# Planning the stores of gates and gated operands two microseconds behind VectorE's last step

## The chip, the cores and the metric

The kernel runs on one core of one Trainium2 chip. The metric is the device time of one execution in microseconds. A core has TensorE (PE: matmuls, PEld: its weight loads), VectorE (DVE), ScalarE (ACT), GpSimd (POOL) and SyncE (SP). In this kernel SP issues all transfers, one after the other, in the order in which they were written; each of the other engines also works through its instructions in one order. An instruction that waits for a semaphore holds up what stands behind it on its engine.

## The reference

```python
attn = softmax(q_c @ k_c.T / 8) @ v_c      # chunks of 64 tokens, 8 heads of 64
x  = attn as (8, 576, 512)
xn = (x - mean) / sqrt(var + 1e-6) * g_ln
x  = x + relu(xn @ w_ch1) @ w_ch2          # 512 -> 2048 -> 512
gate = sigmoid(sum_k conv_w[k] * x shifted by 4 - k tokens)   # k = 0..4, zeros ahead of each sequence
out  = (gate * (x @ w_val)) @ w_out
```

All is fp32. The kernel splits an operand into a high and a low part (`ACTIVATE` Copy, then a subtraction) and adds up three products of them.

## The kernel before, in words

The 4608 tokens are worked through in nine blocks of 512 (b = 0 to 8). For every block there is attention (units of 128 tokens, `unit`), the feed-forward part, and the convolution that makes the gate. Blocks 0 and 1 go through `ffn`. From block 2 on, the first product of the feed-forward is done by `hidden` as seven products of quadrants ("2", "1", "6", "5", "3", "7", "4") for each of four groups g, 12 matmuls of 256 columns a product (L1255). Their weights were put into DRAM (`a_dram[g, m]`) and are loaded again for each product (L1327, in the trace `late_a<-a`, in the order `late_a...<-a3_1` for group 3, part 1) into a ring of six rooms. ScalarE copies a product's sum out (`c_hh`, `c_hl`, L1347), VectorE adds another to it (L1354), and later products wait for that.

`conv(b)` runs for block b while the next block is in `hidden`. For each of four column groups f it makes the gate's sum in u_room, in one of two halves, u0 and u1, in turn: a first step on ScalarE (L1638), four on VectorE (L1645), and a store to `gate_dram` (L1658, `gd`; two transfers where the block holds the start of a sequence). The half is given to the next column group but one when the store has landed. Then `seven` makes the seven operands of the gated part's first product: high on ScalarE (L1472), low on VectorE (L1477), and a store (L1482, `x7d`), from three rooms in turn. For block 0 the same is done later, out of a copy of x in DRAM (`x2d`): `seven_again` loads quadrants into u0 and u1 (L1525) as soon as the stores of the gates there have landed, and `conv_again` makes its gates in the halves too (L1600 is its store). After block 8, `val` and `proj` do the gated part; they load the operands (L1872) and the gates (L1849).

What sets the order: nearly everything is an `Op` of a `Plan`, with engine, an estimated duration, dependences and a priority. `Plan.run` plays them through in time. An engine that is free takes the ready op of the lowest priority number, and the instructions are written in that order, so the plan's times decide the order on each engine and nothing else. An op becomes ready at the end of the last op that it depends on, plus a hop (`HOP`, 80 ns behind VectorE, 3500 behind a store or load on SP), plus that op's `more`, plus its own `slack` behind SP. `HOP` is all that a store got behind VectorE.

Of the kernel before, what the change touches and what calls it, by code (L numbers as in the profile page):

```python
# [20 lines left out]


class Op:
    __slots__ = ("eng", "dur", "fn", "deps", "pri", "left", "after", "ready", "seq", "xfer", "more", "slack")

    def __init__(self, eng, dur, fn, deps, pri, seq):
        self.eng, self.dur, self.fn, self.pri, self.seq = eng, dur, fn, pri, seq
        self.deps = [d for d in dict.fromkeys(deps) if d is not None]
        self.after, self.ready, self.xfer, self.more, self.slack = [], 0.0, None, 0.0, 0.0


class Plan:
# [23 lines left out]
    def run(self):  # L56
        for op in self.ops:
            op.left = len(op.deps)
            for d in op.deps:
                d.after.append(op)  # L60
        free = {e: 740.0 if e == "SP" else 0.0 for op in self.ops for e in op.eng}
        ready = {e: [] for e in free}
        events = []
        done = set()

        def offer(op):
            for e in op.eng:
                heapq.heappush(ready[e], (op.pri, op.seq, op))

        for op in self.ops:  # L70
            if not op.left:
                offer(op)
        t, n, moved, landed = 0.0, 0, 0.0, []
        while n < len(self.ops):
            for e in free:
                if free[e] > t:
                    continue
                q = ready[e]
                while q and q[0][2].seq in done:
                    heapq.heappop(q)  # L80
                if not q:
                    spent = self.idle(t) if self.idle and e == "PE" else None
                    if spent:
                        free[e] = t + spent
                        heapq.heappush(events, (free[e], -1, None))
                    continue
                op = heapq.heappop(q)[2]
                done.add(op.seq)
                dur = op.dur[op.eng.index(e)] if isinstance(op.dur, tuple) else op.dur
                end = t  # L90
                for x, parts in op.xfer or ():
                    flying = landed[-self.LANES :]
                    if len(flying) == self.LANES:
                        end = max(end, flying[0][0])
                    for l, _ in flying:
                        if sum(m for z, m in flying if z > end) + parts > self.RING:
                            end = max(end, l)
                    turn = self.TURN if parts == P and landed and landed[-1][1] != P else 0.0
                    end += dur
                    moved = max(end + self.LAG, moved + turn) + x  # L100
                    landed.append((moved, parts))
                if not op.xfer:
                    end = t + dur
                free[e] = end
                if len(op.eng) > 1:
                    op.fn(e)
                else:
                    op.fn()
                n += 1
                for a in op.after:  # L110
                    if op.xfer:
                        wait = moved - end
                    else:
                        wait = 0.0 if a.eng == (e,) else max(self.HOP[e], self.HOP["PE"] if "PE" in a.eng else 0.0) + op.more
                        if e == "SP":
                            wait += a.slack
                    a.ready = max(a.ready, end + wait)
                    a.left -= 1
                    if not a.left:
                        heapq.heappush(events, (a.ready, a.seq, a))  # L120
                heapq.heappush(events, (free[e], -1, None))
            if n == len(self.ops):
                break
            t = max(t, events[0][0])
            while events and events[0][0] <= t:
                op = heapq.heappop(events)[2]
                if op is not None:
                    offer(op)
# [3 lines left out]
def chunk_attention_ffn_gated_conv(  # L132
# [1299 lines left out]
    def seven(b, quad, reads, pri):  # L1432

        st, last = {}, {}
        HB = NB // 2

        def mix(to, x, y, *deps):


            def side(q):
                return [(0, HB, st["t"][:, :, :HB])] if q is None else list(quad(*q))

            def go():
                if "t" not in st:
                    st["t"] = slot("hl1", [P, 2, HB], F32, f"t{b}")
                many = side(x) if x else side(y)
                for lo, hi, _ in many:
                    o, p, r = (  # L1450
                        [a for l, h, a in side(q) if (l, h) == (lo, hi)] or [st["t"][:, :, lo:hi]]
                        for q in (to, x, y)
                    )
                    nc.vector.tensor_tensor(out=o[0], in0=p[0], in1=r[0], op=ALU.subtract)

            o = add("DVE", 760, go, list(deps), pri)
            for q in (x, y):
                if q:
                    last.setdefault(q, []).append(o)
            return o  # L1460

        def split(i, m, src, *deps):
            rt, sp = SPLITS[n_split[0] % 3], {}
            n_split[0] += 1

            def sources():
                return quad(*src) if src else [(0, HB, st["t"])]

            def high():
                sp["t"] = slot(rt, [P, 2, 2, HB], F32R, f"x7_{b}_{m}")  # L1470
                for lo, hi, a in sources():
                    nc.scalar.activation(out=sp["t"][:, 0, :, lo:hi], in_=a, func=AF.Copy)  # L1472

            def low():
                t = sp["t"]
                for lo, hi, a in sources():
                    nc.vector.tensor_tensor(  # L1477
                        out=t[:, 1, :, lo:hi], in0=a, in1=t[:, 0, :, lo:hi].bitcast(F32), op=ALU.subtract
                    )

            def store():
                nc.sync.dma_start(out=x7_dram[b, m].bitcast(F32), in_=sp["t"].bitcast(F32))  # L1482

            oh = add("ACT", 680, high, list(deps) + take(rt), pri)
            ol = add("DVE", 690, low, [oh], pri)
            x7_store[b, m] = add("SP", 1300, store, [ol], pri)
            x7_store[b, m].more = 2000.0
            hold(rt, x7_store[b, m])
            if src:
                last.setdefault(src, []).append(ol)  # L1490
            return ol

        return mix, split, last
# [77 lines left out]
    def conv_again(f):  # L1571
# [30 lines left out]
        pri = when[4 + f, KF // 2]  # L1602
# [4 lines left out]
            oa = add("DVE", 760, more(i), [oa], pri)  # L1607
        hold(rt, oa)
        conv_store[0, f] = add("SP", 728, keep, [oa], pri)
        hold(at, conv_store[0, f])  # L1610

    def conv(b):
# [19 lines left out]
        for f in range(KD if b else 0):  # L1632
            st = {}
            at = f"u{f % 2}"

            def first(f=f, st=st, at=at):
                st["acc"] = slot(at, [P, XW], F32, f"acc{b}_{f}")
                nc.scalar.activation(  # L1638
                    out=st["acc"][:, :L], in_=X[b][:, f, :L], func=AF.Copy, scale=cw_sb[:, 0, f : f + 1]
                )  # L1640

            def more(i, f=f, st=st):
                def go():
                    a = st["acc"][:, :L]
                    nc.vector.scalar_tensor_tensor(  # L1645
                        out=a,
                        in0=X[b][:, f, i : i + L],
                        scalar=cw_sb[:, i, f : f + 1],
                        in1=a,
                        op0=ALU.mult,  # L1650
                        op1=ALU.add,
                    )

                return go

            def keep(f=f, st=st):
                for lo, hi, c in segs:
                    nc.sync.dma_start(  # L1658
                        out=gate_dram[b][:, f, lo:hi], in_=st["acc"][:, c - P0 : c - P0 + hi - lo]
                    )  # L1660

            oa = add("ACT", 740, first, [oz, cw_op] + done + take(at), pri)
            for i in range(1, KT):
                oa = add("DVE", 760, more(i), [oa], pri)
            last.append(oa)
            conv_store[b, f] = add("SP", 728, keep, [oa], pri)
            hold(at, conv_store[b, f])
        if b == 0:
            x2_store[b] = add("SP", 2900, store, done, pri)
# [441 lines left out]
```

## Time and profile before

| | |
|---|---|
| median of three runs | 1070.41 us (1068.2 to 1075.63) |
| the profiled execution's own time | 1070.03 us |
| its span, from first to last instruction | 1068.2 us |
| TensorE busy | 1053.9 us, 99% |
| VectorE busy | 856.4 us, 80% |
| ScalarE busy | 540.3 us, 51% |
| DMA, mean of the 16 engines | 266 GB/s |

TensorE's granted clock is at full speed in all 40 slices of the page. The waits view says who waited for whom; the timeline lists instructions in order of time with the idle time ahead of them in brackets. For SP a row is the issue of a transfer, not the transfer.

### The profile page before, as it was taken

How to read it: one execution, taken by the hardware profiler on the slowest of the kernel's cores; microseconds unless marked ns; L12 is line 12 of the kernel's file. 1: busy time of each engine (PE TensorE's matmuls, PEld its weight loads, DVE VectorE, ACT ScalarE, POOL GpSimd, SP SyncE). 2: the span in 40 equal slices, each digit the busy share in tenths (PEclk: the TensorE clock that was granted, in tenths of full speed). 3: DMA queues.
4: the chain of work that ended last, by engine and by line, in shares of the span. 5: the costliest groups of instructions: out<-in, count | busy, mean ns of one | idle time of the engine just before them, and what ended most of it. 6: DMA issues, size and time to landing. Idle time of an engine off the chain costs nothing.

```text
span 1068.2 us, 22725 instructions
## 1 busy us (share of the span) xinstructions
PE 1053.9 (99%) x8950; PEld 951.4 (89%) x8950; DVE 856.4 (80%) x1464; ACT 540.3 (51%) x871; POOL 40.4 (4%) x77
## 2 busy tenths in 40 slices
PE   9999999999999999999999999999999999999998
PEld 8988888888899988889888898899898989999998
DVE  5888978888885888767878877878756889998785
ACT  5796634435354445445445543544443555655553
POOL 1011000000000000000000000000000000000000
PEclk9999999999999999999999999999999999999999
DMA  8995358667999899989989989998976988999852
GB/s 193 289 368 175 108 159 252 220 179 207 246 329 270 233 297 337 282 242 344 278 260 329 299 233 233 352 282 250 319 234 203 381 330 305 309 334 377 316 206 80
DMA packets 205905, 284.14 MB, mean 266 GB/s; under 512 B 99278, under 2 KB 151014, under 8 KB 205798
## 3 DMA queue, kind: packets, MB, share of 16 engines
q1 hardware_dynamic: 205798, 282.68, 84.6%
q8 instruction: 71, 1.16, 0.5%
q14 instruction: 36, 0.29, 0.1%
HBM read 207.64 MB, written 67.63 MB: 258 GB/s over the span
## 4 chain that ended last, share of the span: by engine, by line
PE 88%; DMA 4%; issue 2%; DVE 2%; ACT 2%; SPq 1%; POOL 0%; DVEq 0%; ACTq 0%; POOLq 0%
PE m L1255 24%; PE o L1255 8%; PE v L1255 8%; PE y L1034 7%; PE yA L1412 5%; PE yA L1414 5%; PE yB L1412 5%; PE yB L1414 4%; PE yA L1413 4%; PE yB L1413 4%; PE att L631 3%; PE att L604 3%; PE h L1010 3%; PE h L1012 2%; PE h L1011 2%
## 5 line engine op out<-in xcount | busy, mean ns | idle before, releaser
L1255 PEld LDWEIGHTS m<-late,late_a 128*128 128x128 f32 x2352 | 296.3, 188 | 22.5 <-DVE c_hl L1354 6.1
L1255 PE MATMUL m<-late,late_a 128*128 128x256 f32 x2352 | 303.3, 280 | 7.1 <-DMA late_a<-a 3.1
L1645 DVE SCALAR_TENSOR_TENSOR u_room<-X,cw_sb,u_room 128x516 f32<-128x516 f32 (+1 forms) x128 | 95.1, 747 | 10.4 <-ACT u_room L1638 7.9
L1034 PE MATMUL y<-hh,w 128*128 128x512 f32 x224 | 70.9, 398 | 0.0
L1354 DVE TENSOR_TENSOR c_hh<-c_hh,m 128x512 f32<-128x512 f32 x56 | 38.4, 685 | 36.6 <-PE m L1255 22.9
L1347 ACT ACTIVATE c_hh<-m 128x512 f32<-128x512 f32 x56 | 33.4, 596 | 54.9 <-PE m L1255 54.7
L1412 PE MATMUL yA<-late_h,w 128*128 128x512 f32 x148 | 59.4, 401 | 0.0
L1412 PE MATMUL yB<-late_h,w 128*128 128x512 f32 x148 | 59.0, 399 | 0.0
L1414 PE MATMUL yB<-late_h,w 128*128 128x512 f32 x148 | 58.1, 393 | 0.0
L1414 PE MATMUL yA<-late_h,w 128*128 128x512 f32 x148 | 58.0, 392 | 0.0
L1413 PE MATMUL yA<-late_h,w 128*128 128x512 f32 x148 | 58.0, 392 | 0.0
L1413 PE MATMUL yB<-late_h,w 128*128 128x512 f32 x148 | 57.8, 390 | 0.0
L1034 PEld LDWEIGHTS y<-hh,w 128*128 128x128 f32 x224 | 40.8, 188 | 8.4
L1287 ACT ACTIVATE late<-xs 128x512 fp32r<-128x512 f32 x49 | 30.4, 628 | 35.1 <-PE m L1255 20.6
L1010 PE MATMUL h<-xnt,w 128*128 128x512 f32 x112 | 45.4, 405 | 0.0
L770 POOL TENSOR_TENSOR rstd<-ve,neg_half 128x1 f32<-128x1 f32 x36 | 24.7, 687 | 541.8 <-DVE ve L750 541.4
L1012 PE MATMUL h<-xnt,w 128*128 128x512 f32 x112 | 44.2, 395 | 0.0
L1011 PE MATMUL h<-xnt,w 128*128 128x512 f32 x112 | 44.2, 394 | 0.0
L1034 PE MATMUL y<-hl,w 128*128 128x512 f32 x112 | 44.0, 393 | 0.0
L1382 ACT ACTIVATE late_h<-c_hh 128x512 fp32r<-128x512 f32 x38 | 23.9, 630 | 38.9 <-DVE c_hh L1354 38.2
L678 ACT ACTIVATE p<-p 128x512 f32<-128x512 f32 x33 | 20.8, 630 | 41.6 <-DVE p L670 23.6
L699 ACT ACTIVATE pT<-px 128x1024 uint16<-128x1024 uint16 x28 | 38.5, 1374 | 6.3 <-DMA px<-ps 6.1
(272 smaller groups left out, 2440.0 us busy)
## 6 DMA issues: line engine op xcount, KB each, us to landing
late_a<-a SPq DMA_DIRECT2D x196, 512.0 KB, 5.6
x7d<-late_x SPq DMA_DIRECT2D x42, 512.0 KB, 5.9
late_a<-x7d SPq DMA_DIRECT2D x39, 512.0 KB, 5.4
raw<-in_moe_w_ch_dram SPq DMA_DIRECT2D x32, 512.0 KB, 7.6
late<-x7d SPq DMA_DIRECT2D x24, 512.0 KB, 5.5
qk_room<-in_q_dram SPq DMA_DIRECT2D x100, 112.0 KB, 5.2
qk_room<-in_k_dram SPq DMA_DIRECT2D x100, 112.0 KB, 4.1
x7d<-x SPq DMA_DIRECT2D x21, 512.0 KB, 5.6
```

The costliest lines, as they stand in the source:

```text
L699: nc.scalar.activation(out=t.bitcast(U16).rearrange("p (x s) -> p s x", s=2), in_=st["turned"], func=AF.Copy)
L1010: nc.tensor.matmul(ps, wh, xh, start=(kk == 0), stop=False)
L1011: nc.tensor.matmul(ps, wh, xl, start=False, stop=False)
L1012: nc.tensor.matmul(ps, wl, xh, start=False, stop=(kk == KD - 1))
L1034: nc.tensor.matmul(ps, w[:, s], x, start=opens and n == 0, stop=closes and n == 2, skip_group_check=not b)
L1255: nc.tensor.matmul(ps[:, f], l, right(r, k), start=new and f == k == i == 0, stop=k == 1 and i == 2, skip_group_check=True,)
L1347: nc.scalar.activation(out=st[tag], in_=st[into], func=AF.Copy)
L1354: nc.vector.tensor_tensor(out=st[tag], in0=st[tag], in1=y, op=op)
L1412: nc.tensor.matmul(ps, wh, hh, start=opens and f == 0, stop=False)
L1413: nc.tensor.matmul(ps, wl, hh, start=False, stop=False)
L1414: nc.tensor.matmul(ps, wh, hl, start=False, stop=closes and f == 3)
L1645: nc.vector.scalar_tensor_tensor(out=a, in0=X[b][:, f, i : i + L], scalar=cw_sb[:, i, f : f + 1], in1=a, op0=ALU.mult, op1=ALU.add,)
```

## The change

An op gets a number `behind`, 0 where none is set. The plan adds it where the op waits for one of an engine other than SP. It is set to 2000 ns for three kinds of stores: the operands of the gated part (`x7_store`, in `seven`), block 0's gates (`conv_again`) and the other blocks' gates (`conv`). What the kernel computes and how many instructions it has stay the same; only the plan's times change, and with them the order.

```diff
@@ class Op
-        self.after, self.ready, self.xfer, self.more, self.slack = [], 0.0, None, 0.0, 0.0
+        self.after, self.ready, self.xfer, self.more, self.slack, self.behind = [], 0.0, None, 0.0, 0.0, 0.0
@@ Plan.run
                         if e == "SP":
                             wait += a.slack
+                        else:
+                            wait += a.behind
@@ seven
             x7_store[b, m] = add("SP", 1300, store, [ol], pri)
+            x7_store[b, m].behind = 2000.0
             x7_store[b, m].more = 2000.0
@@ conv_again
         conv_store[0, f] = add("SP", 728, keep, [oa], pri)
+        conv_store[0, f].behind = 2000.0
@@ conv
             conv_store[b, f] = add("SP", 728, keep, [oa], pri)
+            conv_store[b, f].behind = 2000.0
```

What it moves, at three places. The first is SP in the convolution of block 5, while block 6 is in group 2. Before:

```order
L1482 DMA x7d5_2_120<-late_x7_1_1_3132 128x1024
L1327 DMA late_a2_0_2_2135<-a3_2_207 128x1024
L1658 DMA gd5_80<-u_room_185 128x320
L1658 DMA gd5_80<-u_room_185 128x192
L1327 DMA late_a2_0_6_2162<-a3_1_208 128x1024
L1482 DMA x7d5_6_122<-x7_5_6_7962 128x1024
L1327 DMA late_a2_0_6_2162<-a3_6_209 128x1024
```

and of the change (line numbers are two to four higher):

```order
L1484 DMA x7d5_2_120<-late_x7_1_1_3132 128x1024
L1329 DMA late_a2_0_2_2135<-a3_2_207 128x1024
L1329 DMA late_a2_0_6_2162<-a3_1_208 128x1024
L1329 DMA late_a2_0_6_2162<-a3_6_209 128x1024
L565 DMA qk_room_148<-in_q_dram 32x4x224 x4
L1662 DMA gd5_80<-u_room_185 128x320
L1662 DMA gd5_80<-u_room_185 128x192
L1484 DMA x7d5_6_122<-x7_5_6_7976 128x1024
```

The last gate store of block 5 has moved behind two weight loads and the loads of q. The second place is VectorE, ahead of the step that closes `c6_1_hl0` (block 6, group 1; the rows with X5 are gate steps of block 5). Before:

```order
L1354 TENSOR_TENSOR c6_1_hh1_7679<-c6_1_hh1_7679,m5_6_1_7686 128x512
L1645 SCALAR_TENSOR_TENSOR u_room_185<-X5_5931,cw_sb_74,u_room_185 128x516 x2
L1354 TENSOR_TENSOR c6_1_hl0_7719<-c6_1_hl0_7719,m1_6_1_7628 128x512
L1385 SCALAR_TENSOR_TENSOR h6_1_0_7673<-c6_1_hh1_7679,h6_1_0_7672 128x2x256
L669 TENSOR_REDUCE mx31_7821<-att31_7769 128x8
```

and of the change:

```order
L1356 TENSOR_TENSOR c6_1_hh1_7679<-c6_1_hh1_7679,m5_6_1_7686 128x512
L1649 SCALAR_TENSOR_TENSOR u_room_185<-X5_5934,cw_sb_74,u_room_185 128x516
L1356 TENSOR_TENSOR c6_1_hl0_7721<-c6_1_hl0_7721,m1_6_1_7628 128x512
L1387 SCALAR_TENSOR_TENSOR h6_1_0_7672<-c6_1_hh1_7679,h6_1_0_7671 128x2x256
L671 TENSOR_REDUCE mx31_7819<-att31_7768 128x8
```

One of the two gate steps has moved further down. The third place is the convolution of block 2, where `seven_again` begins (block 3, groups 2 and 3). On SP, before:

```order
L1658 DMA gd2_77<-u_room_185 128x128
L1658 DMA gd2_77<-u_room_185 128x384
L1327 DMA late_a2_0_2_2135<-a3_2_207 128x1024
L1525 DMA u_room_185<-x2d_84 128x2x256
L1658 DMA gd2_77<-u_room_185 128x128
L1658 DMA gd2_77<-u_room_185 128x384
L1327 DMA late_a2_0_6_2162<-a3_1_208 128x1024
L1482 DMA x7d2_6_101<-late_x7_1_1_3132 128x1024
L1482 DMA x7d2_3_103<-x7_2_3_4672 128x1024
L1327 DMA late_a2_0_6_2162<-a3_6_209 128x1024
L1482 DMA x7d2_4_105<-late_x7_1_1_3132 128x1024
L1327 DMA late_a2_0_3_2489<-a3_5_210 128x1024
```

and of the change:

```order
L1329 DMA late_a2_0_2_2135<-a3_2_207 128x1024
L1662 DMA gd2_77<-u_room_185 128x128
L1662 DMA gd2_77<-u_room_185 128x384
L1528 DMA u_room_185<-x2d_84 128x2x256
L1329 DMA late_a2_0_6_2162<-a3_1_208 128x1024
L1662 DMA gd2_77<-u_room_185 128x128
L1662 DMA gd2_77<-u_room_185 128x384
L1528 DMA u_room_185<-x2d_84 128x2x256
L1329 DMA late_a2_0_6_2162<-a3_6_209 128x1024
L1484 DMA x7d2_6_101<-late_x7_1_1_3132 128x1024
```

Both loads of x2d now follow the gate stores of the same rooms at once; before, the second one came six transfers after its store (it is the row behind the last that is shown). On VectorE at the same place, before (t0 and x7_0_1 read what the two loads bring; mx20 to ve19 are attention):

```order
L1385 SCALAR_TENSOR_TENSOR h3_2_1_4766<-m1_3_2_4599,h3_2_1_4765 128x2x256
L669 TENSOR_REDUCE mx20_4818<-att20_4773 128x8
L670 TENSOR_TENSOR p20_4817<-att20_4773,mx20_4818 128x2x4x64
L722 TENSOR_SCALAR rs19_4559<-rs19_4559 128x8
L723 RECIPROCAL rs19_4559<-rs19_4559 128x8
L740 TENSOR_TENSOR x19_4834<-att20_4773,rs19_4559 128x2x4x64
L747 BN_STATS stat19_4837<-x19_4834 128x6
L749 BN_AGGR mv19_4835<-stat19_4837 128x2
L750 TENSOR_SCALAR ve19_4839<-mv19_4835 128x1
L1454 TENSOR_TENSOR t0_4866<-u_room_185 128x512
L1477 TENSOR_TENSOR x7_0_1_4864<-u_room_185,x7_0_1_4864 128x512
L1354 TENSOR_TENSOR c3_3_hh0_4768<-c3_3_hh0_4768,m2_3_3_4851 128x512
```

and of the change:

```order
L1387 SCALAR_TENSOR_TENSOR h3_2_1_4766<-m1_3_2_4599,h3_2_1_4765 128x2x256
L1479 TENSOR_TENSOR late_x7_1_1_3132<-t2_4409,late_x7_1_1_3132 128x512
L1456 TENSOR_TENSOR t0_4827<-u_room_185 128x512
L1479 TENSOR_TENSOR x7_0_1_4822<-u_room_185,x7_0_1_4822 128x512
L671 TENSOR_REDUCE mx20_4838<-att20_4773 128x8
L672 TENSOR_TENSOR p20_4837<-att20_4773,mx20_4838 128x2x4x64
L1479 TENSOR_TENSOR late_x7_1_1_3132<-t0_4827,late_x7_1_1_3132 128x512
```

t0 and x7_0_1 have moved from behind the attention steps to ahead of them.

## Rows read from the trace of the kernel before

**Rows 1.** The page: span, and busy time of each engine.

```profile
span 1068.2 us, 22725 instructions
PE 1053.9 (99%) x8950; PEld 951.4 (89%) x8950; DVE 856.4 (80%) x1464; ACT 540.3 (51%) x871; POOL 40.4 (4%) x77
```

**Rows 2.** Waits of TensorE, 235 to 870 us: total us, times, longest us.

```profile
PE m L1255 <- DMA late_a<-a: 3.1, 2, 1.6
PE m L1255 <- DVE c_hl L1354: 2.1, 3, 1.0
PE m L1255 <- DVE hl L1022: 1.4, 1, 1.4
PE m L1255 <- DVE c_hh L1354: 0.5, 1, 0.5
```

**Rows 3.** Waits of SP's queue, 235 to 870 us.

```profile
SPq L1327 <- PE m L1255: 139.0, 92, 4.1
...
SPq L1482 <- DVE late_x L1477: 9.8, 12, 1.8
SPq L1658 <- DVE u_room L1645: 9.7, 7, 2.4
...
SPq L1525 <- DMA gd<-u_room: 3.3, 1, 3.3
```

**Rows 4.** Timeline of SP, 645 to 680 us: start us, us, what.

```profile
667.95 0.59 SPq L1327 DMA_DIRECT2D late_a<-a  x1
670.99 0.86 SPq L1658 DMA_DIRECT2D gd<-u_room  x2
671.95 0.44 SPq L1327 DMA_DIRECT2D late_a<-a  x1
```

**Rows 5.** Timeline of all engines, 650 to 657 us; idle time in brackets.

```profile
654.07 1.55 DVE L1645 SCALAR_TENSOR_TENSOR u_room<-X,cw_sb,u_room 128x516 f32<-128x516 f32 x2 [2.58 <-ACT u_room L1638]
...
656.27 0.97 PE L1255 MATMUL m<-late,late_a 128*128 128x256 f32 x6 [0.78 <-DVE c_hl L1354]
```

**Rows 6.** Timeline of TensorE, 555 to 566 us.

```profile
563.51 1.68 PE L1255 MATMUL m<-late,late_a 128*128 128x256 f32 x12 [0.38 <-DVE c_hl L1354]
```

**Rows 7.** Timeline of SP, 380 to 402 us.

```profile
383.28 1.10 SPq L1658 DMA_DIRECT2D gd<-u_room  x2
384.47 1.48 SPq L1327 DMA_DIRECT2D late_a<-a  x1
389.31 0.38 SPq L1525 DMA_DIRECT2D u_room<-x2d  x1
389.78 0.89 SPq L1658 DMA_DIRECT2D gd<-u_room  x2
390.77 0.42 SPq L1327 DMA_DIRECT2D late_a<-a  x1
...
395.96 0.45 SPq L1525 DMA_DIRECT2D u_room<-x2d  x1
```

**Rows 8.** Line 1525, the loads of x2d: first and last start, landing.

```profile
L1525 SPq DMA_DIRECT2D u_room<-x2d x4: 376/442/997, 389.3 to 425.1; - x4
...
DMA to landing us min/median/max: 6.9/7.3/7.7
```

**Rows 9.** Line 1658, the gate stores: landing.

```profile
DMA to landing us min/median/max: 2.5/4.7/7.6
```

**Rows 10.** Timeline of TensorE, 390 to 425 us.

```profile
396.87 2.98 PE L1255 MATMUL m<-late,late_a 128*128 128x256 f32 x24 [1.61 <-DMA late_a<-a]
...
412.88 1.54 PE L1255 MATMUL m<-late,late_a 128*128 128x256 f32 x12
...
421.06 1.68 PE L1255 MATMUL m<-late,late_a 128*128 128x256 f32 x12
```

**Rows 11.** Timeline of VectorE, 399 to 424 us.

```profile
401.12 0.68 DVE L669 TENSOR_REDUCE mx<-att 128x8 f32<-128x512 f32 x1
...
404.63 0.69 DVE L1454 TENSOR_TENSOR t<-u_room 128x512 f32<-128x512 f32 x1
```

More of the change, by code (lines that the diff above doesn't have):

```diff
@@ L23 @@
 class Op:
-    __slots__ = ("eng", "dur", "fn", "deps", "pri", "left", "after", "ready", "seq", "xfer", "more", "slack")
+    __slots__ = ("eng", "dur", "fn", "deps", "pri", "left", "after", "ready", "seq", "xfer", "more", "slack", "behind")
     def __init__(self, eng, dur, fn, deps, pri, seq):
```

## The prediction

> **What bounds the kernel now.** I read the page first: the profiled execution spans 1068.2 us and TensorE is busy for 1053.9 of it [rows 1]. So 14.3 us are without a matmul. A change that only moves instructions can't shorten the 1053.9: the matmuls are the same in number and shape. It can only take away, or add, time in which TensorE waits.
>
> Second, the waits of TensorE between 235 and 870 us, the stretch of the blocks 2 to 8, in which the gates and the operands of the gated part are made [rows 2]. There are four rows, 3.1 + 2.1 + 1.4 + 0.5 = 7.1 us. The 1.4 us, for hl of L1022, belong to block 1's plain feed-forward; the new order leaves every row up to there as it was. That leaves 5.7 us that the change could remove at best: 1070.03 - 5.7 = 1064.3.
>
> Third, the waits of the transfer queue in the same stretch [rows 3]. SP issues everything in one order. Most of its waiting is for rooms that TensorE has to free (L1327, 139.0 us), which is wanted. The rest is what the change is about: stores of gates stand waiting for VectorE's last step (L1658, 9.7 us in 7 times, 2.4 at most), and so do stores of operands (L1482, 9.8 us in 12 times). While SP stands at such a store, the weight loads (late_a) behind it are not issued.
>
> **What the change does to the plan.** No work is added or removed. In the planner's reckoning each of these stores becomes ready 2000 ns later behind VectorE. Whatever else is ready by then is put ahead of it, on SP and, because u0 and u1 come free later, on VectorE and ScalarE too. I went through the places where TensorE waits now and looked in the new order for what stands there.
>
> *Place one, 668 to 678 us (the first pieces of the order shown above).* The load of a3_1 is issued at 671.95, behind a gate store that SP holds from 668.5 (667.95 plus 0.59) to 670.99 [rows 4]. TensorE waits for it: the two waits for late_a are 3.1 us, the longest 1.6 [rows 2], and this is the other one, 1.5. In the new order the loads of a3_2, a3_1 and a3_6 follow each other and the gate store comes behind them. SP then issues a3_1 at about 668.6 (667.95 plus 0.6), some 3.3 us earlier. That covers 1.5 twice. **Gain 1.5.**
>
> *Place two, 654 to 656 us.* ScalarE's first step of a gate waits for the landing of the gate store before, VectorE's next two steps of that gate start at 654.07 and take 1.55, and only then comes c_hl, for which TensorE waits 0.78 [rows 5]. In the new order one of the two steps stands ahead of c_hl, not two. c_hl comes 1.55 / 2 = 0.78 earlier. **Gain 0.7.** The same happens a block earlier: of four gate steps ahead of c_hl two are left, and two operand steps take VectorE's idle time before them. TensorE waits there for c_hh, 0.5 [rows 2], and for c_hl, 0.38 [rows 6]. c_hh still has to come behind a gate step whose store is now issued one load later, so I keep its wait; the 0.38 goes. **Gain 0.4** (bounds: nothing and 0.9).
>
> *Place three, 383 to 422 us: the cost.* Here two loads of x2d into u_room (L1525) have to wait until the gate stores that read u_room have landed. Before: gate pair issued at 383.28 to 384.38, load of a3_2 to 385.95, then SP stands 3.3 us until 389.31 [rows 3, 7], so this store took 4.9 us to land. The median of all gate stores is 4.7 (2.5 to 7.6) [rows 9]. Then a gate pair, then the load of a3_1 at 390.77. TensorE waits 1.61 us for it [rows 10]. The second load of x2d goes out at 395.96 with six transfers between it and its store: it hardly waits.
>
> In the new order the load of a3_2 is ahead of the gate pair, and each x2d load is directly or one load behind its store. Step by step: a3_2 is issued between 383.2 (SP is free then) and 384.47 (as before) and takes 1.48, the pair 1.10, landing 4.9, so the first x2d load goes out at 390.7 to 392.0 instead of 389.31. With 0.4 for it, the load of a3_1 ends its issue at 391.6 to 392.9 against 391.19. TensorE's wait of 1.61 grows by 0.4 to 1.7; I take **1.0 lost**. Then the second pair (0.89), landing 4.9, and the second x2d load is issued at 397.9 to 399.2, not 396.4. Its landing takes 6.9 to 7.7 [rows 8], median 7.3: 405.2 to 406.5.
>
> VectorE needs that load for the step t0 (404.63 before) [rows 11]. In the new order t0 and the operand step behind it stand ahead of the softmax of unit 20 (mx at 401.12 before) [rows 11]. VectorE reaches t0 at about 402 and stands 3 to 4.5 us; mx comes at 406.4 to 407.7. Queued behind: the eight steps from mx to t0 (3.5 us before), one operand step, then c_hh, which ends at 411.2 to 412.5. The product that needs c_hh runs at 412.88, plus 1.0 of shift [rows 10]: hidden by 1.4 us or more. Some 15 steps, about 9.7 us at the 0.6 to 0.7 that most such steps take, lie between c_hh and c_hl (0.7). So c_hl ends at 421.6 to 422.9, and its product stands at 421.06 plus 1.0 [rows 10]. Stall 0 to 0.9. The loads of v and a3_4 behind the third x2d load are in the same state, late by about as much, so I price the place at 0 to 2.0 and take **0.8 lost**, nearer the lower end because SP's queue is shorter after standing and its transfers land sooner.
>
> A figure of the Trainium skill would make this cost vanish. Its page "DMA: Bandwidth & Descriptors", section "Latency and other measured facts", puts the fixed cost of a transfer at about 2 us; with 256 KB over 16 engines I estimate 2.6 us from that page. By it the first x2d load would not be later than before, t0 would not stall VectorE, and the sum would be 1070.0 - 2.6 = 1067.4 instead of 1069.2. The trace has 4.7 as the median and 2.5 as the least, so I go by the trace.
>
> Elsewhere (the convolutions of blocks 1, 3, 6, 7 and 8) stores move behind loads too, but TensorE waits there for nothing now, or for c_hl once more (2.1 less the two waits above, 0.9) at a place in block 4 where the order stays as it was. I cost that at nothing. What covers it: a room is filled as soon as TensorE frees it (the 92 waits of L1327, [rows 3]), six products ahead of its use. If that cover went at one place, it would cost about the 1.5 us of place one.
>
> **The sum.** 1070.03 (own time; 0.4 under the median of the runs, 1070.41, and inside their 1068.2 to 1075.63) - 1.5 - 0.7 - 0.4 + 1.0 + 0.8 = 1069.2 us.
>
> **The rivals.**
> 1. *All waits go.* Place three is covered after all (stores land early, as in the skill's figure) and the waits left over go with the new order. For it: SP's waits at stores are the common cause of most of them. Against: the x2d loads are now closer to the stores than before. Time: between 1067.4 (losses nothing) and 1064.3 (all 5.7 us). From there on there is nothing more to win.
> 2. *Slower: VectorE stands at t0 and TensorE pays for it.* Everything behind t0 comes 5.3 to 6.6 us later; if the products don't have the cover that I read, place three costs up to 1.7 + 5.6 = 7.3 (the 6.6 less the 1.0 of shift that TensorE has anyway) instead of 1.8, and the time is 1070.03 - 2.6 + 7.3 = 1074.7. It decides from the point where the second x2d load lands later than 406.5. For it: VectorE is busy for 80% of the span [rows 1], so it makes up slowly. Against: 1.4 us of cover at c_hh and the shift that a3_1 gives. To be slower than 1081 it would have to happen at both pairs of x2d loads (the other two follow, the last at 425.1 [rows 8]), 2 x 7.3 - 2.6 = 12.0: 1082.
> 3. *It does nothing.* The planner's lateness is larger than 2 us, so stores still block. Against: the longest wait is 2.4 us and the mean 1.4 [rows 3], and at place one the loads are ahead of the store whatever VectorE does. Time 1070, or 1071.8 with the losses alone.
>
> **How the numbers follow.** Forecast, 1067.4 to 1071.8 (gains partly eaten by place three): 0.58. Rival 1, 1064.3 to 1067.4: 0.15. Rival 2, 1071.8 to 1075: 0.19; above that, 0.08, of which 0.05 over 1081. Under 1064.3 nothing. I give the range 1064.3 to 1075.0, which leaves out 0.08, and rests on the bounds above: no removable wait left, and place three uncovered. One per cent, about what a measurement of this kernel can tell from no change, is 10.7 us: faster than 1059.7 is not to be had from 5.7 us of waits, so 0.01; slower than 1081.1, 0.05; the same, 0.94.
>
> **What will show it.** In the profile of the changed kernel: matmuls busy for 1053 to 1054 us again; no wait of TensorE for late_a near 676 us; SP's waits at the gate stores down from 9.7 us to 3 or less; the wait for c_hl near 655 gone. At 395 us a wait for late_a of 2 to 3.3 us, SP standing twice for some 4 us at L1528 (the x2d loads), and VectorE idle for 3 us or more before t0. If that idle time isn't there, the landing time was wrong; if TensorE waits for c_hl or an att product near 420 us for more than 2 us, the cover was. Wrong altogether would be a new wait at a place where I costed nothing: then this reading by places missed what the new order does to ScalarE's and VectorE's queues.

## The result and the profile after

The changed kernel takes 1076.46 us (median of 20 runs, 1071.96 to 1081.19), the kernel before in the same runs 1069.57 us (median of 20, 1066.25 to 1075.63). The ratio is 1.0068, with a 95% interval of 1.0056 to 1.008: **7.3 us slower (6.0 to 8.6)**. The two medians alone are 6.9 us apart; the text goes by the ratio on record. The forecast was 1069.2 us, and the range ended at 1075.0. The time lies outside the range, and the sign is the other one.

The profiled execution took 1075.5 us, 5.5 more than that of before. The page of after, against [rows 1]:

```profile
span 1073.7 us, 22721 instructions
PE 1056.9 (98%) x8950; PEld 954.3 (89%) x8950; DVE 857.5 (80%) x1464; ACT 540.9 (50%) x871; POOL 40.0 (4%) x77
```

Who TensorE waited for between 235 and 870 us, as in [rows 2] (releaser, us in total, times, longest):

```profile
PE m L1257 <- DMA late_a<-a: 4.9, 3, 3.7
PE att L606 <- DVE xn L791: 1.6, 1, 1.6
PE m L1257 <- DVE hl L1024: 1.4, 1, 1.4
PE att L633 <- DMA v<-in_v_dram: 1.3, 1, 1.3
PE m L1257 <- DVE c_hl L1356: 1.0, 1, 1.0
PE m L1257 <- DVE c_hh L1356: 0.2, 1, 0.2
```

The sum is 10.4 us instead of 7.1. Two rows are new, xn and v, and the longest wait for a weight load is 3.7 us. And TensorE is busy for 3.0 us more, with the same 8950 matmuls: it ran at the lower level of its clock for a while. Both come together at one place, near 585 us:

```profile
583.67 1.54 PE L1257 MATMUL m<-late,late_a 128*128 128x256 f32 x12
588.88 3.32 PE L1257 MATMUL m<-late,late_a 128*128 128x256 f32 x14 [3.67 <-DMA late_a<-a]
```

```profile
core 0: us, PE busy (x), PEclk, DMA share, GB/s
586.00:588.00 2.00, 0.00 (x0) 0.82 1.03 397
588.00:590.00 2.00, 1.12 (x5) 0.50 1.03 417
590.00:592.00 2.00, 2.00 (x11) 0.50 1.02 417
592.00:594.00 2.00, 2.00 (x11) 0.50 0.92 375
594.00:596.00 2.00, 2.00 (x69) 0.97 0.52 160
```

The first fence is TensorE's timeline, the second the windows of 2 us (PEclk is the granted clock: 1.00 is 2.4 GHz, 0.50 is 1.2). TensorE waits 3.67 us for the load of a3_1 (block 5), then works at 1.2 GHz until about 594. At half speed 5.1 us of work lose some 2.6. That is 3.7 us of waiting and 2.6 of slower matmuls at one place, more than the whole difference of the two profiled executions. It was the obvious culprit, and the first experiments were made for it.

SP's waits in the same stretch, against [rows 3]:

```profile
SPq L1329 <- PE m L1257: 157.8, 104, 5.1
SPq L1484 <- DMA late_a<-a: 12.5, 8, 2.2
SPq L1528 <- DMA gd<-u_room: 7.4, 2, 4.7
...
SPq L1662 <- DVE u_room L1649: 2.7, 4, 1.0
```

The change does what it says: SP stands 2.7 us at the gate stores for VectorE, not 9.7, and at the stores of operands 0.9 us for VectorE's low part instead of 9.8 (it stands 12.5 us there for weight loads to land, 3.9 before). But at the x2d loads (L1528) it stands 7.4 us in two pieces instead of 3.3 in one. Place three in SP's timeline, against [rows 7] (a row is the issue; the idle time between rows is SP standing):

```profile
383.60 0.32 SPq L1329 DMA_DIRECT2D late_a<-a  x1
384.01 1.08 SPq L1662 DMA_DIRECT2D gd<-u_room  x2
389.82 0.38 SPq L1528 DMA_DIRECT2D u_room<-x2d  x1
390.29 0.42 SPq L1329 DMA_DIRECT2D late_a<-a  x1
390.80 2.20 SPq L1662 DMA_DIRECT2D gd<-u_room  x2
395.74 0.37 SPq L1528 DMA_DIRECT2D u_room<-x2d  x1
396.21 0.42 SPq L1329 DMA_DIRECT2D late_a<-a  x1
396.68 0.42 SPq L1484 DMA_DIRECT2D x7d<-late_x  x1
...
```

From 385.1 to 389.8 and from 393.0 to 395.7 nothing is issued. Behind the second gap stand three stores of block 2's operands (the first is the last row, two more follow by 398.7), and what they hold shows on ScalarE, VectorE and TensorE:

```profile
402.82 0.63 ACT L1474 ACTIVATE late_x<-t 128x512 fp32r<-128x512 f32 x1 [3.96 <-DMA x7d<-late_x]
403.49 0.69 DVE L1479 TENSOR_TENSOR late_x<-t,late_x 128x512 fp32r<-128x512 f32 x1 [3.90 <-ACT late_x L1474]
404.22 0.69 DVE L1456 TENSOR_TENSOR t<-u_room 128x512 f32<-128x512 f32 x1
410.75 0.54 DVE L791 TENSOR_SCALAR xn<-x,mv,rstd 128x512 f32<-128x512 f32 x1
411.35 0.66 PE L606 MATMUL att<-ident,xn 128*128 128x128 f32 x4 [1.64 <-DVE xn L791]
421.84 1.25 PE L633 MATMUL att<-v,pT 64*64 64x64 f32 x31 [1.27 <-DMA v<-in_v_dram]
```

ScalarE waits 3.96 us for a store of operands to land and free its room; VectorE, whose next step needs that operand, stands 3.90 us; the layer norm of a unit (xn) comes late by that, and TensorE waits 1.64 us for it and later 1.27 us for v.

### The profile page after: what moved, and what is told of

Read it like the earlier page. It is cut to its first block, busy times and chain, and to the rows that moved or that the text cites. A ratio compares the mean times of both kernels' runs of the same rounds, so it can differ in the third digit from the quotient of the medians.

```text
span 1073.7 us, 22721 instructions
## 1 busy us (share of the span) xinstructions
PE 1056.9 (98%) x8950; PEld 954.3 (89%) x8950; DVE 857.5 (80%) x1464; ACT 540.9 (50%) x871; POOL 40.0 (4%) x77
## 4 chain that ended last, share of the span: by engine, by line
PE 90%; DMA 6%; DVE 2%; SPq 1%; issue 0%; ACT 0%; DVEq 0%; ACTq 0%
PE m L1257 23%; PE o L1257 8%; PE v L1257 8%; PE y L1036 7%; PE yA L1414 5%; PE yA L1416 4%; PE yA L1415 4%; PE yB L1414 4%; PE yB L1416 4%; PE yB L1415 4%; PE att L633 3%; PE att L606 3%; DMA late_a<-a 3%; PE h L1012 3%; PE h L1014 2%; PE h L1013 2%
## 5 line engine op out<-in xcount | busy, mean ns | idle before, releaser
L1293 DVE TENSOR_TENSOR late<-xs,late 128x512 fp32r<-128x512 f32 x49 | 33.1, 686 | 12.2 <-ACT late L1289 12.2
```

The source lines that it names most:

```text
L1293: nc.vector.tensor_tensor(out=t[:, 1], in0=quadrant(*src), in1=t[:, 0].bitcast(F32), op=ALU.subtract)
```

## The experiments

Each kernel was timed beside the kernel before on the same chip. Ratios are to that; us are the ratio less 1 times the median of the kernel before (1069.6 to 1070.8 us). To see where the time moves I also took, in every profiled execution, the start of one product ("1" of a group) in two stretches: from block 3 group 2 to block 4 group 0 (in before 382.7 to 429.5 us, place three and its tail), and block 6 group 0 to group 1 (617.1 to 640.1). The table says by how much each stretch was longer than in before:

| kernel | ratio (95%) | us | 382.7 to 429.5 | 617.1 to 640.1 |
|---|---|---|---|---|
| changed kernel | 1.0068 (1.0056 to 1.008) | +7.3 | +3.1 | +0.9 |
| E9 changed, again | 1.0079 (1.0052 to 1.0107) | +8.5 | +6.5 | +5.0 |
| E1 changed, without block 4 | 1.0063 (1.0039 to 1.0087) | +6.7 | +6.4 | 0.0 |
| E2 gates of block 4 alone | 1.0017 (0.9994 to 1.004) | +1.8 | +0.5 | 0.0 |
| E3 block 5 alone | 1.0016 (0.9996 to 1.0036) | +1.7 | +1.7 | 0.0 |
| E4 block 2 alone | 1.0036 (1.0018 to 1.0054) | +3.9 | +3.9 | 0.0 |
| E5 changed, without block 2 | 1.003 (1.0012 to 1.0047) | +3.2 | +3.1 | +3.6 |
| E6 without 2, 4 and 5 | 0.9987 (0.9971 to 1.0003) | -1.4 | +2.1 | 0.0 |
| E7 before, x2d loads later | 0.998 (0.9964 to 0.9997) | -2.1 | +0.3 | +0.4 |
| E8 changed, x2d loads later | 0.9994 (0.9978 to 1.001) | -0.6 | -1.9 | +0.9 |
| E10 block 2 alone, x2d later | 0.9961 (0.9943 to 0.9979) | -4.2 | -1.9 | 0.0 |
| E11 without 4, 5, x2d later | 0.9973 (0.9957 to 0.9989) | -2.9 | -1.9 | 0.0 |
| E12 without 2, 4, 5, x2d later | 0.9978 (0.9962 to 0.9993) | -2.4 | -1.0 | 0.0 |
| E13 E5, one store moved | 1.0002 (0.9982 to 1.0022) | +0.2 | +2.5 | +2.0 |
| E14 E8, one store moved | 1.0011 (0.999 to 1.0032) | +1.2 | -1.9 | +2.4 |

One execution decides little in the last two columns; what counts is that kernels of one order agree. In the first of them even the kernels that have before's order at this place (E2, E3, E5, E6, E13) are 0.5 to 3.1 us longer than before's profile; with before, the six average 1.6. So that profile was a lucky one there.

**Is it the wait at 585 us?** E1 takes the 2 us away from block 4, whose gate stores had slid in front of that load.

```diff
-            x7_store[b, m].behind = 2000.0
+            x7_store[b, m].behind = 0.0 if b in (4,) else 2000.0
-            conv_store[b, f].behind = 2000.0
+            conv_store[b, f].behind = 0.0 if b in (4,) else 2000.0
```

> The changed kernel with the 2 us taken away from the stores of block 4 alone (its gates and its operands); the order up to 553 us is that of the changed kernel. Theory A (one new wait: in block 4's convolution a pair of gate stores slid in front of the load of a3_1 for block 5, which had 0.7 us to spare before; TensorE waits 3.7 us for it and then runs at half clock for about 6.6 us, 3.0 us of extra busy time): the 6.7 us go and the 0.4 us gained near 562 us come back as a loss, so about 1076.5 - 6.3 = 1070.2 us, no wait for late_a near 585 us, granted clock 1.000. Theory B (the loss is spread over place three and many small delays of transfers, and the profiled execution shows only where it fell once): at least 1074 us.

Measured 1.0063 (6 executions). The wait was gone from the profile, and the lost time was not. Theory A falls. E2 sets the 2 us for the gates of block 4 and nothing else:

```diff
+            conv_store[b, f].behind = 2000.0 if b in (4,) else 0.0
```

> The kernel before with the 2 us on one kind of store in one block, the gates of block 4. On SP the order differs from before in four places, all between 553 and 590 us. Theory A: the wait for a3_1 near 585 us and the low clock behind it are there, about 1069.6 + 6.7 - 0.4 = 1075.9 us. Theory B: within 1.5 us of the kernel before. Theory C (the operands' stores do it, not the gates'): as B.

Measured 1.0017: no 6 us here either. The profile has no wait for late_a at that place, but one for c_hl of 1.47 us. And the changed kernel, run once more (E9, unaltered), has only 1.13 us there:

> The changed kernel once more, unaltered, for a second profiled execution. If the wait for a3_1 near 585 us belongs to the order (theory A of the first runs): it is there again, 3 us or more, with low clock behind it. If it fell there by chance: a wait below 1.5 us there, and the lost time elsewhere; the place-three loss (from 390 to 430 us, TensorE's start of block 4 against before) is there in both: 2 to 4 us.

Who TensorE waited for in E9, 235 to 870 us:

```profile
PE m L1257 <- DMA late_a<-a: 5.4, 5, 2.4
PE m L1257 <- ACT c_hl L1349: 2.3, 1, 2.3
...
PE att L633 <- DMA v<-in_v_dram: 1.3, 1, 1.3
```

The 2.4 us are at 395 us, place three, the 2.3 at 634. So the 3.67 us were one execution's. A wait for this load came in other profiles too, also with block 4 as before (2.2 us in E11). What both profiles of the changed kernel share is place three (+3.1 and +6.5 us, where 2 to 4 were expected).

**Are the gains real?** E3 sets the 2 us for block 5 alone; E4 for block 2 alone, place three. E3 was meant to have places one and two. Its trace has place one's order, but at place two VectorE still takes two gate steps ahead of c_hl, as before: it tests place one alone.

```diff
+            x7_store[b, m].behind = 2000.0 if b in (5,) else 0.0
+            conv_store[b, f].behind = 2000.0 if b in (5,) else 0.0
```

> The kernel before with the 2 us on the stores of block 5 alone; the order is that of before up to 654 us. If the gains of places one and two are real and were only covered up by a loss elsewhere: no wait for late_a near 676 us and none for c_hl near 655 us, 1069.6 - 2.2 = 1067.4 us. If what is gained at a wait is given back at the next one: 1069 to 1070 us.

Measured 1.0016, where 0.9979 was expected for a real gain; the profile still has both waits (0.8 us for late_a, 1.0 for c_hl). E4 is the same with (2,):

> The kernel before with the 2 us on the stores of block 2 alone, the block of place three. The prediction's 1.8 us for this place, and the 1.9 us that the waits between 390 and 425 us add up to in the changed kernel against before: about 1071.4 us. If place three costs much more than one profile shows (the prediction's second rival): 1074 us or more. If it costs nothing: 1069.6 us.

Measured 1.0036, twice what the prediction had for the place. TensorE's timeline in E4 shows that a stall there can cost more than the wait:

```profile
415.93 0.66 PE L606 MATMUL att<-ident,xn 128*128 128x128 f32 x4 [2.12 <-DVE xn L791]
416.34 0.48 PE L1414 MATMUL yB<-h,w 128*128 128x512 f32 x1
...
418.29 2.64 PE L1257 MATMUL m<-late,late_a 128*128 128x256 f32 x12
422.84 1.54 PE L1257 MATMUL m<-late,late_a 128*128 128x256 f32 x12
```

It waits 2.12 us for xn, and then a product of 12 matmuls takes 2.64 us that takes 1.54 a little later: low clock, 1.7 us lost by the windows (the granted clock is 0.81, 0.50 and 0.84 in the three windows of 2 us from 416 to 422).

**All but one block.** E5 leaves block 2 out, E6 blocks 2, 4 and 5 (the edit of E1 with (2,) and with (2, 4, 5)).

> The changed kernel with the 2 us taken away from block 2's stores alone, so that the order at place three (383 to 422 us) is that of the kernel before. Theory A (each place adds its own loss, place three the 2.6 us of block 2 alone): 1.0068 - 0.0024 = about 1.0043 of before. Theory B (losses don't add; what one place loses is made good in the next blocks, as the 2.2 us that the run with block 4's gates alone lost at 583 us and had back by 680): 1.006 and above. Theory C (place three carries nearly all): 1.001 or less. In the profile: no wait for xn of L791 near 410 us, TensorE's start of block 4 later than in before by less than 2 us (it was 3.2 later within the changed kernel).

> The changed kernel with the 2 us taken away from the stores of blocks 2, 4 and 5; blocks 0, 1, 3, 6, 7 and 8 keep them. The prediction costed these at nothing. If that holds: 1.000 of before, within 0.002. If they carry a good part of the loss: 1.003 or more.

E5 took 1.003: without block 2 some 4 us of the 7.3 are gone. Its profile has no wait for xn, as expected. Its stretch at place three is still 3.1 us longer than in before: that execution waited 2.50 us for the load of a3_1 there (before 1.61), with low clock behind it. E6 took 0.9987, so the 2 us on blocks 0, 1, 3, 6, 7 and 8 cost nothing.

**Place three's cause.** E7 and E8 give the four x2d loads 4 us of slack, in the kernel before and in the changed one:

```diff
-            o.more = 1500.0
+            o.more, o.slack = 1500.0, 4000.0
```

> The kernel before with 4 us of slack on the four loads of x2d in the second pass over block 0: the plan puts the first of them behind the next gate pair and the load of a3_1, so SP has something to issue while the gate's store lands. Theory A (place three's wait comes from SP standing at the x2d load): the 1.6 us wait for a3_1 near 395 us goes, and with it the low clock that follows it in some executions: 0.9985 to 0.997 of before, 1067.5 to 1069 us where before has 1070.8. If the room freed by TensorE sets the load of a3_1, nothing changes: 1.000.

> The changed kernel with the same 4 us of slack on the loads of x2d. Theory A: place three's loss of 2.6 us goes and the 1.6 us of before's own wait too: 1.0068 - 0.0024 - 0.0015 = 1.003 of before. Theory B (losses there have other causes: VectorE's queue): 1.006 as the changed kernel.

E7 took 0.998, E8 0.9994. The slack gives the kernel before 2.1 us and the changed kernel 7.9 (1.0068 less 0.9994), more than theory A asked. SP in E8 at place three:

```profile
384.13 1.86 SPq L1662 DMA_DIRECT2D gd<-u_room  x2
386.47 0.32 SPq L1329 DMA_DIRECT2D late_a<-a  x1
386.88 0.97 SPq L1662 DMA_DIRECT2D gd<-u_room  x2
389.22 0.32 SPq L1329 DMA_DIRECT2D late_a<-a  x1
391.24 0.38 SPq L1528 DMA_DIRECT2D u_room<-x2d  x1
391.71 0.42 SPq L1484 DMA_DIRECT2D x7d<-late_x  x1
...
395.06 1.11 SPq L1528 DMA_DIRECT2D u_room<-x2d  x1
```

Both gate pairs and both weight loads are out before the first x2d load, the operands' stores are issued at 391.7 instead of 396.7, and SP's waits at the x2d loads for gate stores are down to:

```profile
SPq L1528 <- DMA gd<-u_room: 1.6, 1, 1.6
```

TensorE has no wait at all between 380 and 432 us there. E10 asks it for block 2 alone (E4 with the slack):

> The kernel before with the 2 us on block 2's stores alone and 4 us of slack on the loads of x2d. Theory A (all of block 2's loss is SP standing at the x2d loads, directly behind the gate stores): as the kernel before with the slack, 0.998 of before (0.9965 to 0.9995). Theory B (the stores' places themselves cost): 1.0016, the 0.998 plus the 0.0036 of block 2 alone.

Measured 0.9961 against E4's 1.0036: later gate stores in block 2 cost nothing once the x2d loads don't stand behind them. It is also the fastest kernel of the study, 4.2 us (2.2 to 6.1) under the kernel before, though not clear of E7, E11 and E12. E11 and E12 look for the rest:

> The changed kernel with the slack on the x2d loads, and the 2 us taken away from blocks 4 and 5. With blocks 4 and 5 it took 0.9994 of before. If these two cost what they did alone (1.7 us each) also with place three mended: 0.9994 - 0.0032 = 0.996. If what they cost went with place three: 0.9994. Taken with the next one it also shows block 2's cost with the slack: none, so the same as that within 0.0015.

> The candidate: slack of 4 us on the x2d loads, the 2 us on the stores of blocks 0, 1, 3, 6, 7 and 8 alone. If the two gains add (0.998 for the slack, 0.9987 for these blocks): 0.9967 of before, 1067 us where before has 1070.5. If they are the same time won twice: 0.998.

E11 took 0.9973 and E12 0.9978; the gain of E6 does not add to that of E7, and block 2 is free. E8 less E11, blocks 4 and 5, is 2.2 us, with an uncertainty as large.

**What blocks 4 and 5 cost.** The last column of the table says where: block 6 group 0. All four executions with block 4's operands and gates and block 5's set (changed, E9, E5, E8) lose 0.9 to 5.0 us there, and of the nine without them eight lose nothing and E7 0.4. Block 4 is needed for it: E1, which leaves out block 4 alone, loses nothing there. By its time, though, E1 is only 0.5 us better than the changed kernel, with an uncertainty of some 3 us. In E5:

```profile
620.22 0.37 SPq L1603 DMA_DIRECT2D gd<-u_room  x1
621.16 1.27 SPq L692 DMA_TRANSPOSE px<-ps  x1
628.64 1.34 ACT L701 ACTIVATE pT<-px 128x1024 uint16<-128x1024 uint16 x1 [4.97 <-DMA px<-ps]
629.85 0.56 ACT L1349 ACTIVATE c_hl<-m 128x512 f32<-128x512 f32 x1
630.47 0.74 PE L1257 MATMUL m<-late,late_a 128*128 128x256 f32 x4 [2.54 <-ACT c_hl L1349]
```

ScalarE stands 4.97 us for a transposition of unit 29 (px), which SP issued behind a gate store of block 0, and c_hl is behind it. E13 and E14 move that store alone behind px, in E5 and in E8:

```diff
-        conv_store[0, f].behind = 2000.0
+        conv_store[0, f].behind = 5000.0 if f == 1 else 2000.0
```

> The run without block 2 (1.003 of before), with 5 us instead of 2 on one store, the second gate store of block 0: on SP it moves from ahead of the load of a0_4 and px29 to behind them; nothing else moves on SP or VectorE. Theory D (this store in front of px29 is what blocks 4 and 5 cost): px29 lands earlier, the wait of 2.5 us for c_hl near 628 us goes, and with its low clock up to 4 us: 0.999 to 1.001 of before. If not: 1.003 as without this edit, and a wait near 628 us of 1.5 us or more still there.

> The changed kernel with the slack on the x2d loads (0.9994 of before) and the same one store moved behind px29. Theory D: as without blocks 4 and 5, 0.9973 of before. If not: 0.9994.

E13 took 1.0002 instead of 1.003, E14 1.0011 instead of 0.9994. ScalarE's wait for px is 2.5 us instead of 5.0 in E13 and TensorE's 0.83 instead of 2.54, but E14 still has 1.22 us and no gain. The stretch still loses 2.0 and 2.4 us. (The low clock that the expectation speaks of followed this wait in E9, not in E5.) So the place is shown, but the one store is at most a part of it; the rest of the cause stays open. Two things were not tested. In E13 and E14 a weight load still goes out ahead of px, which goes ahead of it in before. And all six profiles with this loss, none of the ten others, have this wait of ScalarE between 608 and 645 us:

```profile
ACT p L680 <- DVE rs L724: 2.9, 1, 2.9
```

In these six, VectorE takes a gate of block 0 and then the softmax of this unit some 5 us later against TensorE: what px reads is ready 1.0 us ahead of the product named 1 of group 0, and 5.0 us ahead of it in the ten others.

## Why the prediction was wrong

Three steps failed. Place three was mis-sized (1.8 us lost, measured 3.3 to 5.8) because the wait that costs there is another one than the prediction followed; the gains of places one and two were hardly there to be had; and block 4 with block 5, costed at nothing, cost 2.2 to 4.6 us.

*The bound, and that only waits could change.* PE busy was to be 1053 to 1054 us again; it was 1056.9. The prediction left out that a wait can cost its own length once more: behind some of them TensorE works at 1.2 GHz for a while. In E4 2.12 us of waiting cost 1.7 us more, near 585 us 3.67 cost 2.6. This raised the price of every stall, but does not make the difference of the two kernels by itself: a granted clock below 1.000 was noted in 79 of 114 executions of the kernel before and 18 of 24 of the changed one, and those at 1.000 lie 6 us apart as well (means 1069.4 and 1075.6; six executions of the changed kernel).

*Place one (1.5 gained).* SP did what was forecast: the load of a3_1 was issued 8.0 us ahead of its product instead of 4.7 (the wait taken off), 3.2 us earlier, and the first profile of the changed kernel has no wait near 676 us. But the term held the time to landing fixed at what it was before. For this one load, in before, the changed kernel and E1:

```profile
DMA to landing us min/median/max: 6.1/6.1/6.1
DMA to landing us min/median/max: 7.9/7.9/7.9
DMA to landing us min/median/max: 9.5/9.5/9.5
```

In the eight profiles with the order of before it took 4.9 to 6.5 us, in the eight in which the load goes ahead of the gate store 7.0 to 9.5. There it is issued 0.6 to 1.2 us behind the load of a3_2 instead of 2.8 to 4.0; whether that is the reason was not tested. So the earlier issue gained nothing. TensorE waited for this load 0.4 us on average in the first eight (1.5 in before, nothing in four) and 0.6 in the others (1.5 in E1, 1.2 in E5, 0.9 in E9). E3, which has this gain alone, measured +1.7 us (-0.4 to +3.9). The 1.5 that the prediction wanted to win was mostly that one execution's.

*Place two (0.7 gained) and block 4 (0.4 gained): right mechanism.* At place two none of the six profiles with one gate step ahead of c_hl waits for it. But of the ten with two steps only before (0.8 us) and E3 (1.0) do, so there were 0.2 us to be gained on average. In block 4 the five profiles with two steps all wait, 0.3 to 0.7 us, and the eleven with one do not: this gain came as forecast.

*Place three (1.8 lost): right place, wrong link, wrong size.* SP stood twice (4.7 and 2.7 us), VectorE stood 3.9 us (3 to 4.5 predicted) and the softmax came 4 us late, as written. But the 3.9 is right by luck. The second x2d load was not late: it went out at 395.74 (395.96 before) and landed 3.2 us later, not the 7.3 of [rows 8] that the sum used; VectorE waited 0.4 us for the loads of x2d. ScalarE and VectorE stood for a room. The stores of operands behind the second gap were issued from 396.7 on, the first of them 5.4 us later than before, and the next operand had to wait until one had landed. Nor did the wait ahead of the product of a3_1 near 395 us grow (1.0 lost in the sum): it is 0.6, 1.4, 2.2 and 2.4 us in the four profiles that have this order, and 1.6 to 2.5 in the six with that of before (in E1 and E2 what came last was not the load but a step of VectorE).

What TensorE paid for, the prediction did not follow. I followed c_hh and c_hl [rows 10, 11], which indeed had cover; xn of unit 19 stands between them, with 1.4 us in before from its end to TensorE's transposition:

```profile
409.10 0.54 DVE L789 TENSOR_SCALAR xn<-x,mv,rstd 128x512 f32<-128x512 f32 x1
411.05 0.60 PE L604 MATMUL att<-ident,xn 128*128 128x128 f32 x4
```

In the changed kernel xn came 1.65 us later, and TensorE came to it 1.3 us earlier, as its wait for a3_1 was 0.6 us and not longer than before. All four profiles wait for xn (0.2 to 2.1 us), and no other does. With v (1.3 us in three of the four) and the low clock the stretch cost 3.1, 6.5, 6.4 and 3.9 us, 5.0 on average, which is 3.3 more than the average of the six with the order of before. By the times: 3.9 us (E4), or 5.8 (E8's 7.9 less E7's 2.1). This is the term that was mis-sized, by a factor of two to three. The second rival (1074.7, priced with 0.19) was nearer in its time, but its condition, a second x2d load that lands after 406.5, did not occur: it landed at 398.9.

*Elsewhere, nothing.* Right for blocks 1, 3, 6, 7 and 8 (E6: -1.4 us, -3.1 to +0.3). Not for block 4 with block 5: 2.2 us (E8 less E11) to 4.6 (E5 less E6), each uncertain by 2 to 3 us, at 617 to 640 us, where stores and weight loads on SP came ahead of a transposition on which ScalarE waits, with c_hl behind it. The cover that I named, a room filled as soon as TensorE frees it, holds for the weight loads and says nothing of px and v on the same queue. Even for a3_1 it was thin: in before that load for block 5 landed at 583.13, 0.7 us ahead of its product. So the sign that the prediction named for being wrong altogether, a new wait where nothing was costed, did show.

*The rest of the signs.* SP's waits at gate stores for VectorE fell to 2.7 us (3 or less predicted). The wait for late_a at 395 us was 0.6 us in the first profile and 2.4 in E9 (2 to 3.3 predicted). The short landing (an estimate of 2.6 us) from the Trainium skill's page "DMA: Bandwidth & Descriptors", section "Latency and other measured facts", which would have taken place three away, is not what this case shows: SP stood 4.7 us for a gate store to land. And the measurement told 0.7% from no change, where the prediction put that limit at about one per cent.

With the measured terms the sum would have been: 3.9 to 5.8 (block 2) + 2.2 to 4.6 (blocks 4 and 5) - 1.4 (the others) = 4.7 to 9.0 us, against 7.3 measured. These are differences between kernels of this same study, each with an interval of several us: they fit, but they don't prove the split.

## What to carry to other kernels

On a queue that issues in order, moving a store back pulls everything that depends on it, and the engine that waits for it, behind work that was meant to fill the gap: look for the transfer that has to wait for that store to land, and what stands behind it, before counting what the store no longer blocks. An earlier issue is not an earlier landing: at place one 3.2 us of the first were worth nothing, because the load took longer to land. Holding back the waiting load (4 us of slack on four loads) was worth more than holding back the stores, and made the change free (E8: -0.6 us, -2.4 to +1.1). Waits of 1 us read from one execution are not there for the taking when the times scatter by several us: a gain should be counted only where several executions, or several kernels with the same order at that place, show it, and the obvious culprit of one profile deserves a second profile first.

## What was not expected of the hardware

Low clock behind short waits. In the 16 profiles, nine of the 13 waits of TensorE of 1.8 us or more between 300 and 870 us were followed by a stretch at 1.2 GHz, and two of the shorter ones (1.3 us each, near 422 us). Each such stretch lost 1.6 to 1.7 us of work, and 2.6 us after the wait of 3.67. But the other four (2.2 to 2.5 us, in E2, E5, E6 and E11) were followed by full clock. Kernels in which the x2d loads are later were at a granted clock of 1.000 in 43 of 72 executions, the kernel before in 35 of 114.

Times to landing that move with the order. The same weight load took 4.9 to 6.5 us in one order and 7.0 to 9.5 in the other (place one). And an x2d load that SP issued after standing 2.7 us landed in 3.2 us in the changed kernel, while the least of the kernel before was 6.9 [rows 8]. The prediction did say that transfers land sooner after SP has stood, but reckoned this load with 7.3.
